# Another fixed order for the first fourteen steps of an attention and rational-MLP kernel

## The chip, the core and the metric

The kernel runs on one core of one Trainium2 chip. A core has five engines that work side by side, each through its own instructions in their order: TensorE (PE, matmuls; its weight loads are shown as PEld), VectorE (DVE), ScalarE (ACT), GpSimd (POOL) and SyncE (SP), which here issues nearly all of the DMAs. Engines wait for each other through semaphores. The metric is the device time of one execution in microseconds (us).

## What is computed

```python
# q, k, v: (4, 8, 768, 64)
k_sum = k.reshape(B, H, nb, 32, D).max(axis=3)
v_sum = v.reshape(B, H, nb, 32, D).mean(axis=3)
scores_l = where(|i - j| < 16, scale * q @ k.T, -1e9)
scores_s = scale * q @ k_sum.T + log(32)
a = softmax(concatenate([scores_l, scores_s]))
x = (a @ concatenate([v, v_sum])).transpose(0, 2, 1, 3).reshape(3072, 512)
h = x @ w_in                     # 512 -> 2048
P = a0 + a1*h + a2*h**2 + a3*h**3
Q = 1 + |b0|*|h| + |b1|*h**2
out = (P / (Q + 1e-6)) @ w_out   # 2048 -> 512
```

Each query sees its neighbours within 16 places and 24 block summaries of 32 keys. The result of the attention goes through a two-layer network with a rational function between the layers. The weights arrive as 64-bit numbers.

## The kernel before

**Tiling.** The 3072 rows are cut into six groups of 512 (`NG`), the hidden width of 2048 into sixteen chunks of 128 (`NFC`). One step is one chunk of one group, so there are 96 steps. In a step `moe1` (L390) multiplies the group's x by a chunk of `w_in` into a PSUM tile `h` (12 matmuls: high x high, high x low, low x high part), `gelu` (L402) evaluates the rational function and leaves a high and a low part, `gh` and `gl`, and three steps later (`LAG`) `moe2` (L432) multiplies these by the chunk of `w_out` into `po` (12 matmuls).

**Attention.** It is cut into 48 halves of 64 queries (`jj`). `whole(jj)` (L502) is a generator. Its pieces, one per call, are: score matmuls on PE (`sc`); masked maxima on DVE (`ss`, `sm`); four exponentials on ACT; a reciprocal on DVE (`sm`); the scaling of the probabilities on POOL (`ss`, four instructions); then, once PE has turned them (`turned`, L259, tile `pt`), a copy to SBUF on ACT (`pts`); value products on PE (`av`); a copy of the result on ACT (`x`). Halves 0 to 7, which make group 0, come before step 0; halves 8 to 15, which make group 1, start at steps 0, 1, 3, 4, 6, 7, 9 and 10 (`EARLY_HALF`); the rest follow in pairs after step 14.

**Weights.** `w_split(fc)` (L353) turns a 64-bit chunk into two FP32R parts, high and low. It is a generator of five pieces: a rescaling on ACT (`wr`), the low bits on POOL (`wr`), a merge on DVE (`wr`), the high part by a cast on ACT (`wearly` or `w`), the low part by a subtraction on DVE (`wearly` or `w`). The fifth piece also issues the load of the chunk four further on, into the buffer that it has just read (L386 to L388).

**The function between the layers.** `gelu` has five pieces: square, absolute value and a linear term on ACT (`sq` or `tq`, `ta`, `tu`); the denominator on DVE (`tq`, from `sq` in PSUM or from `tq` in SBUF); logarithm and exponential on ACT (`ta`); three fused operations on DVE (`gh`, `tq`, `tu`); a product on POOL (`gl`). Two further DVE operations on `tu`, which read `h` from PSUM, are called on their own (`products`, L406). The square goes to PSUM in steps 2, 5, 8, 11, 12 and 13 and to SBUF in the others (L414).

**What sets the order.** Three strings. `FIRST` (L48) is the order of the first loads: K keys with their block maxima, Q queries, S constants, F and G value tiles for the block means, W weight chunks, V values, A queries and keys of one half. `EARLY` (L49) orders the halves 0 to 7 and the first weight chunks: s scores and maxima, e the exponentials to the scaling, v block means, p or P the turning with the copy on ACT or DVE, c or C the value products, m the means, k a copy of the block maxima, w a piece of `w_split`. `STEP` (L56) is walked once per step after that step's `moe1`: a letter and a distance back (for w: ahead) name what makes its next piece. g is `gelu`, q the two products, h a half, w a chunk, k the copy of block maxima into `kw`, l and a loads of values and of queries with keys, u reductions of the next batch's keys and their loads, P the second layer with the turning (`moe2`), v block means of the second batch. In steps 0 to 13 (`NSTRICT`) each of PE, DVE, ACT and POOL keeps exactly the order in which the text issues its instructions (`Kept`, L78). SP isn't held by this. From step 14 on, a planner orders the work.

Of the kernel before, what the change touches and what calls it, by code (L numbers as in the profile page):

```python
# [18 lines left out]
B, H, S, D = 4, 8, 768, 64  # L19
# [25 lines left out]
LAG = 3  # L45
SOFF = 12
NWARM = 6
FIRST = "K0 Q0 K1 K2 K3 S F Q1 W0 V0 V1 V2 V3 V4 V5 V6 V7 W1 A8 A9 W2 W3 G"  # L48
EARLY = ("s0 s1 e0 s2 e1 s3 v0 v1 s4 e2 e3 P0 e4 v2 v3 s5 P1 s6 v4 v5 w0 w0 e5 w0 s7 P2 m0 w0 w0 C0 e6 P4 P3 e7 c2 c1 p5 P6 C3 P7 k8 w1 w1 c5 c4 w1 c7 k9 c6 w1 w1 w2 w2")  # L49
AVGW = NK + NB - 4  # L50
NLATE = 4
NSTG = 8
EARLY_HALF = (0, 1, 3, 4, 6, 7, 9, 10)
NSTRICT = NFC - 2
CROSS = 1
STEP = "h3 k0 h0 l0 h1 a0 w2 h1 g1 h3 h0 u w3 g0 w2 g0 q0 h0 w2 g1 w3 q0 P2 v h2 g0"  # L56
NHALF = NT // HQ


# [1 line left out]
def tile_kernel(ctx, tc, qw_in, kraw, kwin, vpad, vred, wio, a, b, cmask, cident, cavg, out):  # L61
# [407 lines left out]
    for i in range(NWARM):  # L469
        pe.matmul(warm, zero[:, 0:P], zero, start=True, stop=True)  # L470
    for what in FIRST.split():
        n = int(what[1:] or 0)
# [34 lines left out]
    chains, by_dve = {}, set()  # L507
    for what in EARLY.split():
        kind, n = what[0], int(what[1:])
# [41 lines left out]
    for step in range(NG * NFC + LAG):  # L551
# [6 lines left out]
        if g < NG:  # L558
# [4 lines left out]
            queue.append((g, fc, (gh, gl)))  # L563
        for what in STEP.split() if strictly else ():
            kind, n = what[0], int(what[1:] or 0)
# [120 lines left out]
```

## Time and profile before

| | us |
|---|---|
| median of three runs | 651.43 (650.79 to 651.48) |
| span of the profiled execution | 647.9 |
| median above the span | 3.5 |
| start of the first h matmul, step 0 | 37.25 |
| start of the h matmuls of step 14 | 144.21 |

The page of the profile gives the span of its execution from the first to the last instruction; what lies around the span is not shown there, so the 3.5 us are simply the difference between the two rows. Over the whole span PE is busy for 624.7 us, DVE for 576.9, ACT for 459.0 and POOL for 257.4. These are averages over stages with different limits: the loads and halves 0 to 7 up to 37 us, the fourteen ordered steps up to about 148 us, and the planned steps after that. All instructions that go through `Kept` carry line L88, so they are told apart by the names of their tiles (output<-inputs). In a timeline a row gives the start, the time taken, the engine, the operation, the tiles and shapes, how many were merged, and in brackets the idle time before it with what ended it.

### The profile page before, as it was taken

How to read it: one execution, taken by the hardware profiler on the slowest of the kernel's cores; microseconds unless marked ns; L12 is line 12 of the kernel's file. 1: busy time of each engine (PE TensorE's matmuls, PEld its weight loads, DVE VectorE, ACT ScalarE, POOL GpSimd, SP SyncE). 2: the span in 40 equal slices, each digit the busy share in tenths (PEclk: the TensorE clock that was granted, in tenths of full speed). 3: DMA queues.
4: the chain of work that ended last, by engine and by line, in shares of the span. 5: the costliest groups of instructions: out<-in, count | busy, mean ns of one | idle time of the engine just before them, and what ended most of it. 6: DMA issues, size and time to landing. Idle time of an engine off the chain costs nothing.

```text
span 647.9 us, 11828 instructions
## 1 busy us (share of the span) xinstructions
PE 624.7 (96%) x4068; PEld 499.4 (77%) x4068; DVE 576.9 (89%) x1152; ACT 459.0 (71%) x1032; POOL 257.4 (40%) x350
## 2 busy tenths in 40 slices
PE   8998879988999999999999999999999999999997
PEld 5666657866788887788888778888788888888886
DVE  4699999999998989988999999988988888988885
ACT  3889869977677577767758677758767756765652
POOL 1855666754243235244233244333334232222221
PEclk9999979989999999999999999999999999999999
DMA  9997644403354435234424332314233110010001
GB/s 322 340 356 263 205 148 157 139 26 107 113 176 116 125 122 160 83 128 150 119 88 141 103 129 93 108 63 130 66 129 114 40 64 1 21 45 1 0 2 65
DMA packets 51559, 77.00 MB, mean 119 GB/s; under 512 B 6068, under 2 KB 33076, under 8 KB 49580
## 3 DMA queue, kind: packets, MB, share of 16 engines
q1 hardware_dynamic: 50796, 75.80, 36.1%
q8 instruction: 32, 0.52, 0.3%
q10 hardware_dynamic: 576, 0.25, 0.1%
q0 software_dynamic: 128, 0.20, 0.1%
q14 instruction: 27, 0.22, 0.1%
HBM read 61.31 MB, written 14.73 MB: 117 GB/s over the span
## 4 chain that ended last, share of the span: by engine, by line
PE 51%; DVE 29%; ACT 7%; issue 6%; POOL 6%; DMA 1%; SPq 0%; DVEq 0%; POOLq 0%
PE po L88 24%; PE h L88 22%; DVE tu L88 10%; DVE tq L88 7%; DVE gh L88 4%; POOL ss L88 4%; ACT ss L88 3%; PE av L88 2%; DVE xl L88 2%; PE sc L88 2%; ACT ta L88 2%; DVE ss L88 2%; DVE ks L88 1%; DMA kres<-in_kraw_dram 1%; PE pt L88 1%
## 5 line engine op out<-in xcount | busy, mean ns | idle before, releaser
L88 POOL TENSOR_TENSOR gl<-tu,ta 128x512 fp32r<-128x512 f32 x96 | 129.1, 1345 | 298.9 <-DVE tu L88 159.6
L88 POOL TENSOR_SCALAR ss<-ss,sm 128x120 f32<-128x120 f32 x192 | 95.2, 513 | 81.6 <-DVE sm L88 79.5
L88 ACT ACTIVATE ta<-tq,cs 128x512 f32<-128x512 f32 x96 | 69.7, 726 | 76.3 <-DVE tq L88 74.7
L88 PE MATMUL po<-wearly,gh 128*128 128x512 f32 x384 | 122.8, 401 | 0.0
L88 PE MATMUL po<-w,gh 128*128 128x512 f32 x384 | 121.7, 398 | 0.0
L88 PE MATMUL h<-xh,wearly 128*128 128x512 f32 x384 | 96.1, 392 | 1.6 <-DVE sm L88 1.1
L88 PE MATMUL h<-xh,w 128*128 128x512 f32 x384 | 95.0, 389 | 0.0
L88 PEld LDWEIGHTS h<-xh,wearly 128*128 128x128 f32 x384 | 71.9, 188 | 18.7 <-ACT wr L88 1.3
L88 ACT ACTIVATE ss<-ss,sm 128x120 f32<-128x120 f32 x192 | 73.2, 384 | 15.4 <-DVE sm L88 15.2
L88 PEld LDWEIGHTS h<-xh,w 128*128 128x128 f32 x384 | 72.0, 188 | 15.2 <-ACT x L88 0.2
L88 PEld LDWEIGHTS po<-w,gh 128*128 128x128 f32 x384 | 71.3, 190 | 16.0 <-issue 1.7
L88 PEld LDWEIGHTS po<-wearly,gh 128*128 128x128 f32 x384 | 70.6, 191 | 16.2 <-issue 2.2
L88 DVE SCALAR_TENSOR_TENSOR gh<-tu,cs,ta 128x512 fp32r<-128x512 f32 x96 | 73.2, 762 | 9.2 <-ACT ta L88 1.2
L88 PE MATMUL po<-w,gl 128*128 128x512 f32 x192 | 75.4, 393 | 0.0
L88 PE MATMUL po<-wearly,gl 128*128 128x512 f32 x192 | 75.4, 393 | 0.0
L88 DVE SCALAR_TENSOR_TENSOR tu<-tu,cs,tq 128x512 f32<-128x512 f32 x96 | 72.9, 760 | 2.5
L88 ACT ACTIVATE tu<-h,cs 128x512 f32<-128x512 f32 x96 | 74.7, 778 | 0.0
L88 DVE SCALAR_TENSOR_TENSOR tu<-tu,cs,h 128x512 f32<-128x512 f32 x96 | 71.3, 743 | 2.3
L88 DVE SCALAR_TENSOR_TENSOR tq<-tq,gh 128x512 f32<-128x512 f32 x96 | 66.3, 691 | 3.0
L88 ACT ACTIVATE ta<-h,cs 128x512 f32<-128x512 f32 x96 | 65.2, 679 | 3.0 <-POOL gl L88 2.9
L88 DVE TENSOR_TENSOR tu<-tu,h 128x512 f32<-128x512 f32 x96 | 64.9, 676 | 0.0
L88 ACT ACTIVATE ta<-ta 128x512 f32<-128x512 f32 x96 | 60.9, 634 | 2.8
(73 smaller groups left out, 925.3 us busy)
## 6 DMA issues: line engine op xcount, KB each, us to landing
wr<-in_wio_dram SPq DMA_DIRECT2D x15, 1024.0 KB
cross<-tb SPq DMA_DIRECT2D x32, 256.0 KB
vw<-in_vpad_dram SPq DMA_DIRECT2D x42, 192.0 KB
kw<-in_kwin_dram SPq DMA_DIRECT2D x40, 192.0 KB
pts<-cross SPq DMA_DIRECT2D x96, 64.0 KB
out_dram<-o SPq DMA_DIRECT2D x24, 256.0 KB
qw<-in_qw_dram SPq DMA_DIRECT2D x40, 128.0 KB
kr<-in_kraw_dram SPq DMA_DIRECT2D x12, 384.0 KB
```

Source lines behind the costliest of these rows:

```text
L88: out = getattr(self.engine, name)(*args, **kw)
```

## The change

Only the three strings change.

```diff
-FIRST = "K0 Q0 K1 K2 K3 S F Q1 W0 V0 V1 V2 V3 V4 V5 V6 V7 W1 A8 A9 W2 W3 G"
-EARLY = ("s0 s1 e0 s2 e1 s3 v0 v1 s4 e2 e3 P0 e4 v2 v3 s5 P1 s6 v4 v5 w0 w0 e5 w0 s7 P2 m0 w0 w0 C0 e6 P4 P3 e7 c2 c1 p5 P6 C3 P7 k8 w1 w1 c5 c4 w1 c7 k9 c6 w1 w1 w2 w2")
+FIRST = "K0 Q0 K1 K2 K3 Q1 S F W0 V0 V1 V6 V2 V4 V5 A9 W1 V7 V3 A8 W2 W3 G"
+EARLY = "s0 s1 e0 s2 s6 e1 s3 s4 P0 v0 v1 e2 e3 e4 v2 v3 s5 P1 v4 v5 w0 w0 e5 w0 s7 P2 m0 w0 w0 C0 e6 P4 P3 e7 c2 c1 k8 p5 P6 C3 w1 P7 w1 c5 c4 w1 c6 c7 k9 w1 w1 w2 w2"
-STEP = "h3 k0 h0 l0 h1 a0 w2 h1 g1 h3 h0 u w3 g0 w2 g0 q0 h0 w2 g1 w3 q0 P2 v h2 g0"
+STEP = "k0 h3 w1 h2 h0 w2 P2 w1 w3 h3 g1 h0 g0 l0 q0 g1 g0 q0 h1 w2 u h0 a0 w3 v g0 h2"
```

Read by engine, a step s changes as follows (a chunk or half is named by its number; s-1 is the step before).

| engine | order before | order after |
|---|---|---|
| PE | h(s), av(s-3), sc(s), pt(s-2) with po(s-3), block means | the same |
| DVE | reciprocal(s-1), merge(s+2), gh tq tu (s-1), maxima(s), reduction, denominator(s), product(s), subtraction(s+2), product(s) | subtraction(s+1), merge(s+2), gh tq tu (s-1), maxima(s), product(s), denominator(s), product(s), reciprocal(s-1), reduction |
| ACT | x(s-3), rescaling(s+3), square to linear (s), cast(s+2), exponentials(s), pts(s-2), logarithm and exponential (s) | rescaling(s+3), x(s-3), square to linear (s), cast(s+2), exponentials(s), logarithm and exponential (s), pts(s-2) |
| POOL | scaling(s-1), gl(s-1), low bits(s+3) | scaling(s-2), gl(s-1), low bits(s+3) |

A chunk's subtraction, and with it the load of a later chunk, moves from step fc-2 to step fc-1, and the scaling of a half from the step after its scores to the second step after, in which PE also turns it.

## The prediction

> **What bounds the kernel now.** First the stretches of time, by busy time of each engine (start and end, length, then busy us of each engine with its instructions, granted clock, DMA share, GB/s):
>
> ```profile
> 60.00:80.00 20.00, 17.46 (x103) 13.41 (x104) 19.86 (x39) 17.13 (x40) 9.51 (x10) 1.00 0.67 222
> ...
> 175.00:644.00 469.00, 465.94 (x2855) 381.42 (x2844) 419.47 (x808) 322.27 (x712) 159.04 (x231) 1.00 0.28 89
> ```
>
> The third figure after the length is DVE. In this sample of the ordered steps it works for 19.86 of 20 us, PE for 17.46 and ACT for 17.13. After 175 us PE works for 465.94 of 469 us. So the ordered steps are bound by DVE, with PE and ACT not far behind, and what comes later by PE. A microsecond gained in the ordered steps therefore brings every later PE instruction forward by a microsecond; nothing in the tail waits for anything else long enough to swallow it.
>
> If DVE is already busy, can an order alone gain anything? Only if its instructions take longer than they need. The groups by line and shape for 37 to 165 us give the mean in ns after the busy time:
>
> ```profile
> L88 DVE TENSOR_TENSOR w<-wr,w 128x1024 fp32r<-128x1024 f32 x7 | 10.6, 1510 | 0.3 <-ACT w L88 0.2
> L88 DVE TENSOR_TENSOR wearly<-wr,wearly 128x1024 fp32r<-128x1024 f32 x7 | 10.5, 1501 | 0.0
> L88 DVE SCALAR_TENSOR_TENSOR tq<-tq,cs,ta 128x512 f32<-128x512 f32 x9 | 9.9, 1101 | 0.6 <-ACT ta L88 0.6
> L88 DVE COPY kw<-ks 128x96 f32<-128x96 f32 x3 | 1.5, 486 | 0.0
> ```
>
> Now DVE's timeline. The first rows run with POOL idle, the rows at 59.16, 66.79 and 122.83 do not:
>
> ```profile
> 42.12 0.75 DVE L88 SCALAR_TENSOR_TENSOR tq<-tq,cs,ta 128x512 f32<-128x512 f32 x1
> 42.78 0.68 DVE L88 TENSOR_TENSOR tu<-tu,h 128x512 f32<-128x512 f32 x1
> ...
> 59.16 2.07 DVE L88 TENSOR_TENSOR wearly<-wr,wearly 128x1024 fp32r<-128x1024 f32 x1
> ...
> 64.44 0.75 DVE L88 SCALAR_TENSOR_TENSOR tu<-tu,cs,tq 128x512 f32<-128x512 f32 x1
> ...
> 66.79 1.60 DVE L88 SCALAR_TENSOR_TENSOR tq<-tq,cs,ta 128x512 f32<-128x512 f32 x1
> 68.31 0.67 DVE L88 TENSOR_TENSOR tu<-tu,h 128x512 f32<-128x512 f32 x1
> 68.91 1.21 DVE L88 TENSOR_TENSOR wearly<-wr,wearly 128x1024 fp32r<-128x1024 f32 x1
> 70.05 0.73 DVE L88 SCALAR_TENSOR_TENSOR tu<-tu,cs,h 128x512 f32<-128x512 f32 x1
> ...
> 70.79 1.19 DVE L88 SCALAR_TENSOR_TENSOR wr<-wr 128x1024 int32<-128x1024 int32 x1
> 71.90 0.74 DVE L88 SCALAR_TENSOR_TENSOR gh<-tu,cs,ta 128x512 fp32r<-128x512 f32 x1
> ...
> 74.08 0.27 DVE L88 CUSTOM_DVE_ANT_0 ss<-sc,mask 128x120 f32<-128x120 f32 x1
> ...
> 74.89 0.95 DVE L88 TENSOR_REDUCE ks<-kr 128x24 f32<-128x768 f32 x1
> 75.75 0.79 DVE L88 SCALAR_TENSOR_TENSOR tq<-tq,cs,ta 128x512 f32<-128x512 f32 x1
> ...
> 86.53 1.23 DVE L88 SCALAR_TENSOR_TENSOR wr<-wr 128x1024 int32<-128x1024 int32 x1
> ...
> 110.60 1.23 DVE L88 SCALAR_TENSOR_TENSOR wr<-wr 128x1024 int32<-128x1024 int32 x1 [0.39 <-POOL wr L88]
> ...
> 122.83 1.65 DVE L88 SCALAR_TENSOR_TENSOR tq<-tq,cs,ta 128x512 f32<-128x512 f32 x1
> ```
>
> And POOL's own rows:
>
> ```profile
> 13.92 1.38 POOL L88 TENSOR_SCALAR ss<-ss,sm 128x120 f32<-128x120 f32 x4 [13.47 <-DVE sm L88]
> ...
> 59.02 1.12 POOL L88 TENSOR_SCALAR wr<-wr 128x1024 int32<-128x1024 uint8 x1
> 65.37 1.30 POOL L88 TENSOR_TENSOR gl<-tu,ta 128x512 fp32r<-128x512 f32 x1 [5.23 <-DVE tu L88]
> 66.76 1.09 POOL L88 TENSOR_SCALAR wr<-wr 128x1024 int32<-128x1024 uint8 x1
> 71.04 3.69 POOL L88 TENSOR_SCALAR ss<-ss,sm 128x120 f32<-128x120 f32 x4 [3.19 <-DVE sm L88]
> ...
> 76.07 1.47 POOL L88 TENSOR_SCALAR wr<-wr 128x1024 int32<-128x1024 uint8 x1
> ...
> 122.65 1.29 POOL L88 TENSOR_TENSOR gl<-tu,ta 128x512 fp32r<-128x512 f32 x1
> ```
>
> The reader is to see a pattern. POOL's `wr` began at 59.02 and DVE's subtraction, which reads two SBUF tiles, at 59.16: 2.07 us instead of 1.21, ending 1.09 after `wr` ended at 60.14. `tq` at 66.79 began just after a `wr` and took 1.60 instead of 0.75; at 122.83 it fell behind `gl` and took 1.65. At 75.75 `tq` was first: it took 0.79, and `wr` was stretched to 1.47. So of a long POOL instruction and a DVE instruction with two SBUF inputs, the later one waits. Operations on `h` in PSUM (0.67, 0.73) don't show it. [...]
>
> Last, two of the things that DVE waited for in 37 to 155 us (total, times, longest); the other two, 0.6 for `ta` and 0.2 for `w`, stand in the groups above:
>
> ```profile
> DVE wr L88 <- POOL wr L88: 1.3, 3, 0.5
> ...
> DVE ss L88 <- PE sc L88: 0.4, 1, 0.4
> ```
>
> The whole pot is: `tq` 9 x (1.10 - 0.75) = 3.2; subtractions 7 x (1.501 - 1.21) + 7 x (1.510 - 1.21) = 4.1; waits 1.3 + 0.6 + 0.4 + 0.2 = 2.5; the three `kw` copies at most 3 x 0.49 = 1.5. Sum 11.3 us.
>
> **The change, part by part.** No instruction is added or removed. The prices of DVE, from start to start in the rows above with POOL out of the way: subtraction 1.14 (68.91 to 70.05), merge 1.11, `gh`, `tq`, `tu` together 2.18 (71.90 to 74.08), maxima 0.81, reduction 0.86, `tq` denominator 0.66 (42.12 to 42.78), product 0.60 (68.31 to 68.91), the second product with a reciprocal 0.74 (70.05 to 70.79), of which I give the reciprocal 0.08.
>
> *Order of DVE and POOL in a step.* I lay the new order out from the start of the subtraction. With maxima: merge at 1.14, `gh` 2.25, end of `tu` 4.5, maxima 4.43, first product 5.24, denominator 5.84, second product 6.50, next step 7.24. POOL's `gl` follows `tu` by about 0.2 (`tu` of 64.44 ended at 65.19, `gl` began at 65.37), so 4.7 to 6.0. The denominator at 5.84 meets its last 0.15 us only, which costs nothing, since after a block it needs some 0.55 (122.83 + 1.65 less 122.65 + 1.29). That is what "maxima and product before the denominator" buys: 3.2 us to 0.1, if those 1.4 us stay in front of it. `wr` then waits for the denominator (6.6) and ends 1.0 later, 7.6, as at 76.07 to 77.54. The next subtraction, wanted at 7.24, ends 1.09 after that: 0.2 late. Without maxima: denominator at 5.03 from PSUM, next subtraction at 6.4, `wr` 6.1 to 7.2: 0.6 late. In steps 1 to 4 the reduction (0.86) now stands last and covers `wr`: nothing late. Steps 5, 8, 11, 12, 13 have no maxima, 6, 7, 9, 10 have: 5 x 0.6 + 4 x 0.2 = 3.8 us remain of the 4.1.
>
> *Waits.* The merge's wait for `wr` (1.3) goes, since the subtraction now stands ahead of it; that of the denominator for `ta` (0.6) is covered by the product before it (0.60); the subtraction's wait for the cast (0.2) by a whole step. The 0.4 in step 0 stays, its order is the same. Gain 2.1. The `kw` copies: no gain taken, 0 to 1.5 possible, since they now open a step beside the end of `wr`.
>
> *A chunk finished one step later.* One subtraction less in step 0, one more at step 14, where DVE has 419 of 469 us to do: nothing. Its load is issued later by up to a step, some 7 us, and must be there two steps on, some 14 us. Of SP's queue the waits for 30 to 150 us show
>
> ```profile
> SPq L251 <- PE av L88: 33.0, 6, 11.8
> ```
>
> A megabyte at the 222 GB/s of the table takes 4.7 us. I take nothing, but 11.8 + 4.7 would be 2.5 us late if a value load stood ahead of it.
>
> *PE and ACT.* From the chain that ended last (start, us, what):
>
> ```profile
> 96.33 0.62 PE av L88 x16
> 96.95 0.97 PE sc L88 x16
> 97.91 2.95 PE po L88 x12
> ...
> 103.59 0.11 PE pt L88
> ...
> 106.81 2.75 PE h L88 x12
> ...
> 110.23 0.37 ACT x L88
> ...
> 117.94 0.34 ACT x L88
> ```
>
> A PE step with everything: 0.62 + 0.97 + 3.22 (103.59 to 106.81, turning and `po`) + 2.75 = 7.6; without turning 7.3; without `av` and `sc` 6.0: 20.9 for three. ACT's full step is 7.7 (110.23 to 117.94), the others about 7.2 and 5.7: 20.6. DVE's three are 7.24 + 7.24 + 6.4 + 1.0 of remaining blocks = 21.9, where it now takes 24.1 (merges of 86.53 and 110.60, three steps apart). DVE stays the longest, with 1.0 us in front of PE. The copy `pts` now comes last on ACT and `av` waits for it; the square-to-linear run needs `x` copied first. By the rows that leaves the linear term ready some 0.6 us before its product asks for it. I take 0, bounded by 0 and 0.4 a full step, 1.6 in all.
>
> *Loads and halves 0 to 7.* The same work. Scores of half 6 come earlier on PE, its exponentials do not; the second queries pass ahead of 1.5 MB of value tiles that are used later. Taken as 0, bounds ±1 (the waits before PE in that stretch are each under 1 us).
>
> Sum: 3.1 + 0.3 + 2.1 = 5.5 us. Against the span: 647.9 - 5.5 = 642.4; the median shown lies 3.5 above the span, carried unchanged: **645.9 us**.
>
> **The rivals.**
>
> *More than that.* If `wr` starts before the subtraction is due in all steps, 3.8 more goes, and `kw` 1.5: 640.6. Against it: `wr` is held back by the denominator.
>
> *The blocks only move: no change.* POOL's `wr` can cost DVE at most one full block a step, 0.86 (row 59.16). Steps 1 to 13 in full: 11.2 us against 3.2 + 4.1 + 2.1 = 9.4 removed. Half a block more than I laid out per step gives 651.4 - 5.5 + 13 x 0.43 = 651.5. What speaks for it: the margin at the denominator is 0.2 us.
>
> *Slower: PE waits for the moved scaling.* Its queue is `wr`, then the scaling, with the turning of the same half in the same step on PE, and `po` and the next `h` behind it. PE has 24.1 - 20.9 = 3.2 us to spare in three steps, which hold two turnings; above 1.6 us of waiting for each the period is longer than before. At 2 us: 20.9 + 4 = 24.9, so 0.8 x 4.5 periods more than now, **655.0**. Against it: the scaling starts at about 0.1 to 0.4 of the step and, at 3.7 us, ends by 4.1, and only its first quarter must be there when the turning starts at about 3.
>
> Long waits of PE cost more:
>
> ```profile
> 86.61 1.86 PE L88 MATMUL sc<-kw,qw 64*64 64x120 f32 x16 [3.60 <-DVE kw L88]
> ```
>
> After 3.60 us of idleness these scores took 1.86 instead of the 0.97 above. [...]
>
> *Slower in another way: the scalings block DVE.* They now stand beside the subtraction and the merge. If each quarter (0.35, a fourth of the 1.38 at 13.92) started first and held DVE up, 8 halves x 1.38 = 11.0 us would come on top: 656.9. Against it: beside the scaling at 71.04 the `gh` at 71.90 and its followers kept their spacing. [...]
>
> *A late load.* It doesn't do what it says where the chunk's data arrive late: one or two waits of 2.5 us leave 648 to 651.
>
> **How the numbers follow.** A measurement of this kernel can tell about 0.2%, 1.3 us. My forecast, 645.9 with its own range of 643.5 to 648.5: 0.42. More (640 to 643.5): 0.16. A late load or part of the gain lost behind step 14 (648.5 to 650.1): 0.12. Blocks only move, 650.1 to 652.7: 0.12. Slower, 655 by PE's waits: 0.13; 657 by the scalings: 0.05. Faster 0.70, same 0.12, slower 0.18. The range: 640.6, the bottom of the pot, to 654; this leaves out about half the slower cases and a little below.
>
> **What would show it.** In the changed profile: `tq<-tq,cs,ta` near 0.75 to 0.85; subtractions still near 1.45 to 1.5; no wait of `wr` on DVE for POOL; three ordered steps about 22 us; `h` of step 14 some 5.5 us earlier than 144.21; the stretch after it as long as before. Wrong: waits of PE's `pt` for POOL `ss`, of ACT's `wr` for its load, `tq` still above 1.0, or a first `h` that moves by more than 1 us.

## The result, and the profile after

| | before | after |
|---|---|---|
| median (lowest to highest, runs) | 651.45 us (650.79 to 651.59, 4) | 646.92 us (645.66 to 648.14, 4) |
| ratio after / before, 95% interval | | 0.9937 [0.9912, 0.9961] |
| span of the profiled execution | 647.9 us | 643.6 us, its own time 645.66 |
| first `gh` to fourteenth `gh` on DVE | 102.22 us (46.37 to 148.59) | 97.50 us (46.69 to 144.19) |

The change saves 4.5 us in the median and 4.3 in the span. The last row is the measure used below: DVE makes `gh` once in each step, so from the first to the fourteenth lie thirteen ordered steps, without what the start of an execution adds before them.

The stretches of time show where the gain sits: start and end, length, then busy us of PE, its weight loads, DVE, ACT and POOL with their instructions, granted clock, DMA share, GB/s. Kernel before, four steps and then nine:

```profile
46.37:80.38 34.01, 29.80 (x182) 21.55 (x179) 33.73 (x64) 30.47 (x64) 21.43 (x21) 1.00 0.71 243
80.38:148.59 68.21, 62.70 (x416) 49.00 (x415) 65.26 (x113) 56.61 (x112) 43.91 (x40) 0.92 0.35 116
```

The changed kernel, the same steps, and the planned part behind them:

```profile
46.69:80.01 33.32, 29.73 (x170) 20.71 (x164) 31.94 (x65) 29.60 (x63) 22.11 (x19) 0.90 0.80 260
80.01:144.19 64.18, 60.12 (x394) 46.42 (x392) 63.55 (x113) 55.71 (x110) 47.26 (x42) 1.00 0.37 127
...
175.00:640.00 465.00, 461.61 (x2809) 377.80 (x2807) 414.81 (x790) 318.83 (x703) 157.74 (x230) 1.00 0.28 88
```

DVE's busy time falls by 1.79 us in the first four steps, but their length by only 0.69: idle time of DVE, which had been 0.28, is 1.38. In the nine steps behind, busy time falls by 1.71 and idle time from 2.95 to 0.63, and the length by 4.03. From 175 us on PE still works nearly all the time.

The groups of the changed kernel by shape, 37 to 158 us (busy us, mean ns of one, idle before), against 1510, 1501, 1101 and 486 before:

```profile
L88 DVE TENSOR_TENSOR w<-wr,w 128x1024 fp32r<-128x1024 f32 x7 | 10.7, 1527 | 0.0
L88 DVE TENSOR_TENSOR wearly<-wr,wearly 128x1024 fp32r<-128x1024 f32 x7 | 8.5, 1217 | 0.1
L88 DVE SCALAR_TENSOR_TENSOR tq<-tq,cs,ta 128x512 f32<-128x512 f32 x9 | 6.9, 769 | 0.0
...
L88 DVE COPY kw<-ks 128x96 f32<-128x96 f32 x3 | 1.8, 597 | 0.0
```

The denominator (`tq`) has lost its stretch. The seven early subtractions (`wearly`) have lost theirs, the seven later ones (`w`) have not, and the small copies `kw` became longer. The timeline says why. DVE's rows:

```profile
84.34 0.83 DVE L88 COPY kw<-ks 128x96 f32<-128x96 f32 x1
85.08 1.21 DVE L88 TENSOR_TENSOR wearly<-wr,wearly 128x1024 fp32r<-128x1024 f32 x1
...
98.55 0.75 DVE L88 SCALAR_TENSOR_TENSOR tq<-tq,cs,ta 128x512 f32<-128x512 f32 x1
...
99.96 1.40 DVE L88 TENSOR_TENSOR w<-wr,w 128x1024 fp32r<-128x1024 f32 x1
...
106.66 1.87 DVE L88 TENSOR_TENSOR w<-wr,w 128x1024 fp32r<-128x1024 f32 x1
```

and POOL's:

```profile
52.09 4.48 POOL L88 TENSOR_SCALAR ss<-ss,sm 128x120 f32<-128x120 f32 x4
...
83.98 1.12 POOL L88 TENSOR_SCALAR wr<-wr 128x1024 int32<-128x1024 uint8 x1
...
97.41 1.30 POOL L88 TENSOR_TENSOR gl<-tu,ta 128x512 fp32r<-128x512 f32 x1 [4.67 <-DVE tu L88]
98.79 1.50 POOL L88 TENSOR_SCALAR wr<-wr 128x1024 int32<-128x1024 uint8 x1
...
106.33 1.13 POOL L88 TENSOR_SCALAR wr<-wr 128x1024 int32<-128x1024 uint8 x1
```

In a step with maxima `gl` ends at 98.71 and `tq`, at 98.55, is clean; `wr` stretches behind `tq` to 100.29 and delays the subtraction of 99.96 by 0.2. In a step without maxima `wr` starts at 106.33, 0.3 before the subtraction, which then takes 1.87. Step 6 opens with the copy `kw`, which takes the blow, 0.83 where it takes 0.20 unhindered (row of 94.57 in the kernel before), and the subtraction at 85.08 is clean.

Last, what PE and DVE waited for from 37 to 152 us (total, times, longest). First DVE:

```profile
DVE ss L88 <- PE sc L88: 1.0, 2, 0.5
DVE gh L88 <- ACT ta L88: 0.3, 1, 0.3
DVE tu L88 <- ACT tu L88: 0.3, 1, 0.3
```

and PE, with a wait that was not there before:

```profile
PE pt L88 <- POOL ss L88: 6.8, 8, 2.2
```

Four of those eight waits, 3.6 of the 6.8 us, stand in one place, the turning in step 2. PE's timeline:

```profile
52.52 0.32 PE L88 MATMUL pt<-ident,ss 128*120 128x128 f32 x1 [0.74 <-POOL ss L88]
55.08 0.47 PE L88 MATMUL pt<-ident,ss 128*120 128x128 f32 x1 [2.24 <-POOL ss L88]
55.85 0.47 PE L88 MATMUL pt<-ident,ss 128*120 128x128 f32 x1 [0.30 <-POOL ss L88]
56.62 0.47 PE L88 MATMUL pt<-ident,ss 128*120 128x128 f32 x1 [0.30 <-POOL ss L88]
56.88 3.62 PE L88 MATMUL vf<-vf,kres 128*120 128x512 f32 x4
...
59.52 3.31 PE L88 MATMUL h<-xh,wearly 128*128 128x512 f32 x8
```

The four scalings, 4.48 us from 52.09 on, are awaited one by one. After that the block means (`vf`) take 3.62 us instead of 1.98 (row of 47.05 in the same timeline), and the next `h` 3.31 instead of 2.40 (48.46). The granted clock is 0.50 from 54.58 to 61.41 us, which makes the 0.90 of the first stretch, and this is the source of DVE's new waits in step 3.

### The profile page after: what moved, and what is told of

The parts are those of the page before. It is cut to its first block, busy times and chain, and to the rows that moved or that the text cites. A ratio compares the mean times of both kernels' runs of the same rounds, so it can differ in the third digit from the quotient of the medians.

```text
span 643.6 us, 11833 instructions
## 1 busy us (share of the span) xinstructions
PE 623.1 (97%) x4068; PEld 497.2 (77%) x4068; DVE 573.3 (89%) x1152; ACT 459.1 (71%) x1032; POOL 259.7 (40%) x350
## 4 chain that ended last, share of the span: by engine, by line
PE 62%; DVE 19%; POOL 7%; ACT 5%; issue 4%; DMA 2%; SPq 0%; DVEq 0%; POOLq 0%
PE po L88 28%; PE h L88 27%; DVE tu L88 7%; POOL ss L88 5%; DVE tq L88 4%; PE sc L88 3%; PE av L88 3%; DVE gh L88 2%; DVE xl L88 2%; ACT ta L88 1%; PE vf L88 1%; DVE ss L88 1%; DMA kres<-in_kraw_dram 1%; POOL gl L88 1%; ACT ss L88 1%
## 5 line engine op out<-in xcount | busy, mean ns | idle before, releaser
L88 POOL TENSOR_SCALAR ss<-ss,sm 128x120 f32<-128x120 f32 x192 | 100.8, 544 | 61.8 <-DVE sm L88 59.1
```

Source lines behind the costliest of these rows:

```text
L88: out = getattr(self.engine, name)(*args, **kw)
```

## The experiments

Theory: a DVE instruction with two SBUF inputs waits for a POOL instruction that reads SBUF, whole instruction for whole instruction, and the order within a step decides which pairs meet. Rivals: the gain comes from the start (loads and halves 0 to 7), or from finishing chunks a step later; or what costs is not the reading but a dependence on POOL's result, or POOL being busy at all. All lengths below are from the first `gh` to the fourteenth in the one profiled execution of each kernel. A ratio is taken against the runs of the kernel before that were made beside that kernel; their medians were 651.45 us for the first result, 651.40 for the four runs from the new start to the denominator first, 651.18 for the repeat and the three from the chunk in its step to the eight matmuls, and 650.06 for the last four.

| run | length us | time us (lowest to highest, runs) | ratio to before, 95% interval |
|---|---|---|---|
| before | 102.22 | 651.45 | |
| changed | 97.50 | 646.92 | 0.9937 [0.9912, 0.9961] |
| changed, again | 97.22 | 646.93 (645.21 to 654.09, 12) | 0.9939 [0.9909, 0.9970] |
| new start alone | 102.91 | 652.18 (650.34 to 657.29, 12) | 1.0014 [0.9985, 1.0043] |
| new step order alone | 97.33 | 645.54 (645.27 to 645.60, 6) | 0.9907 [0.9870, 0.9944] |
| before, product ahead of denominator | 102.25 | 651.57 (649.31 to 654.54, 12) | 1.0003 [0.9978, 1.0028] |
| changed, denominator first | 99.94 | 652.91 (651.12 to 656.77, 12) | 1.0021 [0.9993, 1.0050] |
| changed, chunk finished in its step | 96.33 | 647.67 (644.03 to 653.98, 12) | 0.9928 [0.9901, 0.9955] |
| changed, means before turning | 96.08 | 645.29 (644.00 to 650.20, 12) | 0.9915 [0.9893, 0.9937] |
| changed, eight warming matmuls | 97.27 | 646.13 (645.73 to 647.85, 6) | 0.9925 [0.9898, 0.9953] |
| before, POOL writes zeros | 96.58 | 645.60 (1) | |
| changed, POOL writes zeros | 94.47 | 642.97 (1) | |
| means before turning, eight warming | 96.34 | 645.77 (645.10 to 646.98, 6) | 0.9928 [0.9914, 0.9942] |
| the same, chunk finished in its step | 96.26 | 646.83 (645.34 to 647.20, 6) | 0.9939 [0.9924, 0.9954] |

**The two halves of the change.** The kernel before with the new strings `FIRST` and `EARLY` and the old `STEP`:

```diff
-FIRST = "K0 Q0 K1 K2 K3 S F Q1 W0 V0 V1 V2 V3 V4 V5 V6 V7 W1 A8 A9 W2 W3 G"
+FIRST = "K0 Q0 K1 K2 K3 Q1 S F W0 V0 V1 V6 V2 V4 V5 A9 W1 V7 V3 A8 W2 W3 G"
...
```

> FIRST and EARLY of the changed kernel, STEP of the one before. Theory (the gain comes from the order inside the ordered steps, where a DVE instruction with two SBUF inputs no longer starts behind a long POOL instruction): 651.4 within 1.5, tq<-tq,cs,ta again near 1.1 us. Rival (the loads and halves 0 to 7 bring the gain): about 647, first h matmul earlier than 37.25.

and, the other way round, the old start with the new `STEP`:

```diff
-STEP = "h3 k0 h0 l0 h1 a0 w2 h1 g1 h3 h0 u w3 g0 w2 g0 q0 h0 w2 g1 w3 q0 P2 v h2 g0"
+STEP = "k0 h3 w1 h2 h0 w2 P2 w1 w3 h3 g1 h0 g0 l0 q0 g1 g0 q0 h1 w2 u h0 a0 w3 v g0 h2"
```

> FIRST and EARLY of the kernel before, STEP of the changed one. Theory: all of the gain, 646.9 within 1.5, tq<-tq,cs,ta near 0.77 us. Rival (loads and halves 0 to 7): about 651.

The denominator's group in the first of them, and then in the second:

```profile
L88 DVE SCALAR_TENSOR_TENSOR tq<-tq,cs,ta 128x512 f32<-128x512 f32 x9 | 11.4, 1269 | 0.0
```

```profile
L88 DVE SCALAR_TENSOR_TENSOR tq<-tq,cs,ta 128x512 f32<-128x512 f32 x9 | 7.0, 774 | 0.0
```

The new start alone has the old length and no gain in time, with a `tq` that is even longer than the 1.1 us expected; the new step order alone has the whole gain. The start is worth nothing that these runs can tell.

**One pair exchanged.** In the kernel before the product is put ahead of the denominator and nothing else:

```diff
-STEP = "h3 k0 h0 l0 h1 a0 w2 h1 g1 h3 h0 u w3 g0 w2 g0 q0 h0 w2 g1 w3 q0 P2 v h2 g0"
+STEP = "h3 k0 h0 l0 h1 a0 w2 h1 g1 h3 h0 u w3 g0 w2 q0 g0 h0 w2 g1 w3 q0 P2 v h2 g0"
```

> The kernel before with one swap in STEP: the first product ahead of the denominator (q0 before the second g0). Theory: tq<-tq,cs,ta falls to 0.75 to 0.9 in the steps with maxima, but POOL's low bits then run into the subtraction, which follows at once and grows; net gain 0 to 1.5 us, 650 to 651.5. Rival (the swap alone is the gain, blocks are simply gone): about 648.

The two groups:

```profile
L88 DVE TENSOR_TENSOR w<-wr,w 128x1024 fp32r<-128x1024 f32 x7 | 13.4, 1908 | 0.0
...
L88 DVE SCALAR_TENSOR_TENSOR tq<-tq,cs,ta 128x512 f32<-128x512 f32 x9 | 8.7, 965 | 0.0
```

`tq` fell by 9 x 0.14 = 1.2 us and the `w` subtractions rose by 7 x 0.40 = 2.8 (`wearly` gave 0.7 back), DVE's waits became shorter, and the length is the same to 0.03 us. The block that was not let run out found the next instruction with two SBUF inputs, `w`, 1908 ns instead of 1510. In the changed kernel the opposite exchange, denominator ahead of product:

```diff
-STEP = "k0 h3 w1 h2 h0 w2 P2 w1 w3 h3 g1 h0 g0 l0 q0 g1 g0 q0 h1 w2 u h0 a0 w3 v g0 h2"
+STEP = "k0 h3 w1 h2 h0 w2 P2 w1 w3 h3 g1 h0 g0 l0 g0 q0 g1 q0 h1 w2 u h0 a0 w3 v g0 h2"
```

> The changed kernel with the swap undone: the denominator ahead of the first product (g0 before q0). Theory: in the eight steps with maxima tq<-tq,cs,ta ends about 0.55 later than it could, near 1.25 us, the subtraction behind it is no longer blocked in those steps; loss 1.5 to 3 us, 648.5 to 650. Rival (the earlier subtraction and the later scaling bring the gain, not the place of the denominator): 646.9 within 1.

```profile
L88 DVE SCALAR_TENSOR_TENSOR tq<-tq,cs,ta 128x512 f32<-128x512 f32 x9 | 10.2, 1137 | 0.6 <-ACT ta L88 0.6
L88 DVE TENSOR_TENSOR w<-wr,w 128x1024 fp32r<-128x1024 f32 x7 | 9.7, 1387 | 0.0
```

`tq` is back above 1.1 us and the ordered steps are 2.4 us longer. The median rose by more, 6.0 us, beyond the 1.5 to 3 expected. The profiled execution took 655.29 us, and its span is 9.9 us longer than the changed kernel's: 4.0 of that lie before the first `h` (41.53 us instead of 37.51, see the last section), 2.4 in the ordered steps and 3.5 behind them. Why the planned part became longer was not tested, so only the 2.4 are put down to the exchange.

**The deferral alone.** Every chunk is finished in its step again, the rest of the new order stays:

```diff
-STEP = "k0 h3 w1 h2 h0 w2 P2 w1 w3 h3 g1 h0 g0 l0 q0 g1 g0 q0 h1 w2 u h0 a0 w3 v g0 h2"
+STEP = "k0 h3 h2 h0 w2 P2 w3 h3 g1 h0 g0 l0 q0 g1 g0 q0 h1 w2 u w2 h0 a0 w3 v g0 h2"
```

> The changed kernel with a chunk finished one step earlier again: its subtraction is now the last of a step instead of the first of the next, so that DVE's order from step to step is the same but for the chunk number. Theory: the step's delay is worth nothing, only the subtraction's place is: first to fourteenth gh 97.5 within 0.7 (one subtraction more falls into it, 1.1 us, at its begin, before the first gh), whole time as in the repeat within 1.5. Rival (finishing later gives slack to cast and load and is part of the gain): 1.5 us or more slower than the repeat, with waits of DVE for ACT's cast.

The time did not move beyond its scatter (647.67 against 646.93 in the repeat of the changed kernel beside it). The ordered steps became 0.9 us shorter than in that repeat, and their 96.33 us lie outside the 97.5 within 0.7 that was expected. The repeat, for the scatter of starts and times:

> The changed kernel once more, beside the next three on one chip. From the first gh of DVE to the fourteenth it needs 97.5 us (102.2 before); that will repeat within 0.5. The whole time also depends on the start: in executions whose PE clock falls to half between 10 and 20 us, the first h matmul comes some 4 us later. 645.5 to 647 if the start keeps its clock, 649 to 651 if not.

The 0.9 us are not the deferral's. The second and third of the thirteen steps together, in the repeat and then with each chunk finished in its step:

```profile
59.70:76.40 16.70, 16.04 (x97) 10.98 (x98) 16.07 (x28) 13.55 (x28) 10.70 (x10) 0.82 0.69 227
```

```profile
60.19:75.72 15.53, 14.72 (x90) 10.37 (x92) 15.39 (x28) 13.16 (x27) 11.05 (x10) 0.89 0.77 245
```

They differ by 1.17 us; over the last nine steps the kernel without the deferral is 0.3 us longer (64.42 against 64.13). PE's waits at the turning of step 2 are alike in both: the four turnings start 5.82, 7.26, 8.56 and 9.33 us after the first `gh` in the repeat, and 5.82, 7.25, 8.55 and 9.33 in the other. What differs is the granted clock behind them. It is 0.50 for 6.83 us in the repeat (58.92 to 65.75) and for 3.42 us without the deferral (62.39 to 65.81).

**Step 2.** If the awaited scaling eats what the first steps gain, work for PE ahead of the turning should give some back. The block means (`v`) are such work; they are put ahead of the second layer with its turning:

```diff
-STEP = "k0 h3 w1 h2 h0 w2 P2 w1 w3 h3 g1 h0 g0 l0 q0 g1 g0 q0 h1 w2 u h0 a0 w3 v g0 h2"
+STEP = "k0 h3 w1 h2 h0 w2 v P2 w1 w3 h3 g1 h0 g0 l0 q0 g1 g0 q0 h1 w2 u h0 a0 w3 g0 h2"
```

> The changed kernel with the block means (v) ahead of the turning (P2) in a step. In step 2 PE waits 3.3 us for the moved scaling, then runs at half clock, and DVE waits 0.3 to 0.5 us three times in step 3. Theory: the means fill that wait; first to fourteenth gh falls by 0.5 to 1.2 us from 97.5. Rival (DVE's queue hides this wait as well): 97.5 within 0.2.

PE's timeline in that kernel, the same place:

```profile
52.59 1.88 PE L88 MATMUL vf<-vf,kres 128*120 128x512 f32 x4
...
54.91 0.33 PE L88 MATMUL pt<-ident,ss 128*120 128x128 f32 x1 [0.34 <-POOL ss L88]
56.21 0.32 PE L88 MATMUL pt<-ident,ss 128*120 128x128 f32 x1 [0.98 <-POOL ss L88]
56.98 0.32 PE L88 MATMUL pt<-ident,ss 128*120 128x128 f32 x1 [0.45 <-POOL ss L88]
57.09 2.08 PE L88 MATMUL h<-xh,wearly 128*128 128x512 f32 x8
```

The means run while the first scalings are done; three waits of 1.77 us together are left of the four of 3.6, the granted clock stays at 1.00, and the next `h` takes 2.08 us instead of 3.31. First to fifth `gh` is 31.91 us (47.66 to 79.57), 1.41 less than in the changed kernel, and that is the whole difference of the two lengths; the waits of DVE in step 3 are gone from its list. So the four steps did lose 1.4 us at this one place. But they take 31.91 us also in the kernel that finishes each chunk in its step, where PE waits as long as in the repeat and only the stretch at half clock is shorter. The 1.4 us are thus the price of the long stretch at half clock, not of the waits alone. Five profiled executions with the means behind the turning have the long stretch of 6.8 us (the changed kernel, its repeat, the new step order alone, eight warming matmuls, zeros written) and one has the short one; with the means in front there is none here, and one of 3.4 us in each of the two kernels with eight warming matmuls. That the place of the means makes the difference is likely from this, but one profile of each kernel doesn't show it.

**What POOL does to DVE.** The direct test leaves POOL's instruction in its place and, nearly, its length, but lets it only write. It leaves out the low three bits of the weights' parts:

```diff
-            gps.tensor_scalar(l32, byte, 1.0 / 32, -15.5 / 32, op0=ALU.mult, op1=ALU.add)
+            gps.memset(l32, 0)
```

> The kernel before, with POOL's piece of a weight chunk (the low bits, `wr`, read from bytes) replaced by a POOL instruction of the same place that only writes zeros to the same tile and reads nothing; the low three bits of the weights' parts are left out by this. My theory (a DVE instruction with two SBUF inputs waits for a POOL instruction that reads SBUF, whole instruction for whole instruction): the subtractions fall from 1.50 to about 1.21 us, the merge no longer waits for POOL, `tq` keeps only what `gl` costs it, and from the first `gh` to the fourteenth on DVE it takes 96 to 99 us instead of 102.2. [...]

> The changed kernel with the same replacement (POOL's low bits of a chunk become a write of zeros; the low three bits of the weights' parts are left out). My theory: the subtractions of the steps without reduction fall from 1.40 to 1.87 us to 1.21, `tq` stays near 0.75, and the length from the first `gh` to the fourteenth falls from 97.5 to 93.5 to 95; beside the same replacement in the kernel before, 2 to 4 us remain, the part of `tq` that `gl` costs. [...]

In the kernel before with that edit, POOL's rows

```profile
58.54 1.07 POOL L88 MEMSET wr<- 128x1024 int32 x1
...
65.42 1.02 POOL L88 MEMSET wr<- 128x1024 int32 x1
...
126.64 1.27 POOL L88 TENSOR_TENSOR gl<-tu,ta 128x512 fp32r<-128x512 f32 x1
```

and DVE's beside them:

```profile
58.82 1.22 DVE L88 TENSOR_TENSOR wearly<-wr,wearly 128x1024 fp32r<-128x1024 f32 x1
...
65.60 0.74 DVE L88 SCALAR_TENSOR_TENSOR tq<-tq,cs,ta 128x512 f32<-128x512 f32 x1
...
127.27 1.73 DVE L88 TENSOR_TENSOR w<-wr,w 128x1024 fp32r<-128x1024 f32 x1
```

The subtraction of 58.82 begins inside a POOL instruction of 1.07 us that only writes, and takes its clean 1.22; the same subtraction took 2.07 us in the kernel before, inside a `wr` of 1.12 that reads. `tq` at 65.60 is clean as well. The subtraction of 127.27 falls into `gl`, which reads, and takes 1.73. For a DVE instruction with two SBUF inputs it is the reading instruction that costs, not POOL's work as such. Both rivals fall: POOL is still busy for 1.07 us there and the merge still takes its result, so either would have left the subtraction near 2.07; and the lengths of 96.58 and 94.47 us lie in the ranges of the theory. The copy `kw` doesn't fit this rule. It reads one SBUF tile only and was stretched by the reading `wr`, and in the changed kernel with the edit it still takes 0.59 us at 83.78, inside a writing instruction (83.27 to 84.31), though the subtraction behind it starts 0.10 us later and takes its clean 1.22. The reduction, also with one SBUF input, keeps its 0.92 when it begins inside a reading `wr` (59.04 in the changed kernel). Why the copy differs no run isolates. The groups of this kernel, then those of the changed kernel with the edit:

```profile
L88 DVE TENSOR_TENSOR w<-wr,w 128x1024 fp32r<-128x1024 f32 x7 | 9.7, 1384 | 0.0
L88 DVE SCALAR_TENSOR_TENSOR tq<-tq,cs,ta 128x512 f32<-128x512 f32 x9 | 9.7, 1076 | 0.0
```

```profile
L88 DVE TENSOR_TENSOR w<-wr,w 128x1024 fp32r<-128x1024 f32 x7 | 8.4, 1204 | 0.0
...
L88 DVE SCALAR_TENSOR_TENSOR tq<-tq,cs,ta 128x512 f32<-128x512 f32 x9 | 7.0, 782 | 0.1
```

Without a `wr` that reads, the old order loses 5.6 us of length and the new order 3.0. Of the 4.7 between the two orders 2.1 remain, 3.0 in the last nine steps (64.95 against 61.98) less 0.9 in the first four, where the new order still has its stretch at half clock. What remains is put down to `gl`, which hits `tq` and `w` in the old order (9.7 us each) and hardly in the new (7.0 and 8.4). The subtractions of the old order, too, fell only to 1.38 and 1.29 us, not to the 1.21 expected.

**More warming, and the edits together.** Eight warming matmuls in place of six, alone and with the means ahead of the turning, and the latter with the deferral undone:

```diff
-NWARM = 6
+NWARM = 8
```

> The changed kernel with eight instead of six warming matmuls (NWARM). Theory for the start: PE stays busy until the keys have landed, the clock no longer falls, first h matmul at 37.5 to 38.5 in every execution, 645.5 to 648 with a spread under 2 us. Rival (the late landing of the keys itself sets the start, the clock only follows): spread as before, first h as often at 41 to 42.

> The changed kernel with the block means ahead of the second layer in a step and with eight warming matmuls in place of six: the two edits that each came out a little faster alone. My theory (the means are DVE work that fills a gap, 1.4 us in the ordered steps; the longer warming keeps the start from falling to half clock in the executions in which it does): median 644 to 645.5, a narrower spread of the times than with six (under 3 us from lowest to highest), ratio to the kernel before 0.988 to 0.992. Rival (the spread of the start is not set by the warming): median 645 to 647 with a spread of 5 us or more.

> The one before with the weight chunks finished in the same step again, the deferral undone. My theory (the deferral is worth nothing, in either direction): ordered steps within 1 us of the run before this, time within 0.2% of it. Rival (the deferral covers the subtraction's wait for the cast or the late `wr`): 1 to 3 us longer, with waits of DVE for ACT's cast of 0.5 us or more in the ordered steps.

Warming changes no length. The times of the three kernels with eight scatter by 1.9 to 2.1 us, those with six that ran beside the first of these by 6 to 10 us (changed kernel again, chunk in its step, means first); but beside the other two the kernel before, with six, scattered by only 1.95 us (649.74 to 651.69), and the new step order alone, with six, by 0.33. So whether the warming narrows the times stays open. The two edits together came out at 645.77 us, above the 644 to 645.5 expected. The last two give the deferral no price in the ordered steps, 96.26 against 96.34 us; their times are 1.1 us apart in its favour, within their scatter. The lowest median of the study outside the zero-writing kernels is that of the means first, 645.29 us; its interval overlaps that of the changed kernel, so its times show no gain, and the 1.1 to 1.4 us of length are those of the stretch at half clock.

## Why the prediction was right, and where not

The forecast of 645.9 us lies 1.0 below the median measured, and by span 642.4 lies 1.2 below 643.6. The 3.5 us that were carried from span to median are 3.3 here. Only 2.06 of them lie between this execution's own time and its span; the rest is that the profile caught an execution faster than the median. It did so before, too (the other runs of the kernel before lie 1.8 us above their spans), and that this repeated is luck. Step by step:

**DVE bounds the ordered steps, and POOL's reading instructions stretch it.** Right, and shown by the zero-writing pair. Three ordered steps take 22.24 us (merges of 86.21 and 108.45), as forecast. Two readings behind it were loose. The rows given for operations on `h` in PSUM, 68.31 and 70.05, ran while POOL was idle; one that ran inside a `wr` (76.07 to 77.54) shows the same:

```profile
76.46 0.68 DVE L88 TENSOR_TENSOR tu<-tu,h 128x512 f32<-128x512 f32 x1
```

And the 1.38 us for the four scalings at 13.92, from which the 657 is worked out, don't belong to an idle DVE: until 14.6 it took maxima of scores in PSUM.

**`tq`, -3.1.** Measured 9.9 to 6.9 us, -3.0. Right. One of nine is still hit (0.96 at 67.15).

**Subtractions, -0.3.** Measured 21.1 to 19.2 us for the fourteen, -1.9, but the prediction's 3.8 us of remaining blocks were well sized: 7 x (1.527 - 1.21) = 2.2 remain on `w`, 0.6 + 0.3 fell on the `kw` copies that open steps 6 and 7, in front of the subtraction, and 0.35 on the merge of two half chunks in step 13 (1.72 us where 1.37 is clean in the kernel before). That is 3.5. The gain came out larger than 0.3 because a part of it fell outside the subtractions, and there it was paid: `kw`, taken as 0 with a possible gain, cost 0.6 us more than before over the thirteen steps, and the half chunks' merge 0.35. Together -0.95 in place of -0.3.

**Waits, -2.1.** The merge's wait for POOL (1.3) and the denominator's for `ta` (0.6) went as said. Idle time of DVE over the thirteen steps fell only from 3.23 to 2.01, -1.2, since step 3 got new ones: 0.5 for scores, 0.3 for `ta`, 0.3 for the linear term. They come from PE, the next point.

**PE, taken as 0.** This is the step that failed. The rival in which PE waits for the moved scaling was half there, with 6.8 us in eight waits. It gave 655 with 2 us at every turning; measured were 3.6 us at the turning of step 2 and 3.2 at the other four together, and only the first reached DVE. The prediction let a turning start at about 3 us of the step, amid the second layer's matmuls. In step 2 the second layer, which comes three steps behind, hasn't begun, so the four turnings stand alone and PE waits for each scaling. In the kernel before the granted clock was 0.50 from 85.4 us, still inside the wait of 3.60 us that the prediction shows, to 92.1. Here no wait was longer than 2.24 us, with short matmuls between them, and the clock fell to 0.50 for 6.8 us all the same. The price is 1.4 us, and it hangs on this stretch at half clock: the same waits with half the stretch cost the first four steps nothing. With 1.4 taken off, the length would be 96.1 us, 6.1 gained; with it 4.7 were, instead of 5.5.

**Scalings block DVE, the 657.** Hardly. The scalings are stretched (4.59 us for four at 100.39, 1.38 at 13.92), and the DVE instructions beside them are longer by little: from the first `gh` to the fourteenth the mean of the merge went from 1202 to 1223 ns, that of `gh` from 744 to 761, that of `tq<-tq,gh` from 693 to 720; 12, 13 and 13 of them make 0.8 us against the 11.0 of that rival. Why POOL gives way here and not with `wr` no run isolates. The terms as measured, 3.0 + 0.95 + 1.2 less these 0.8, make 4.4 of the 4.7 us; that the subtractions brought more than forecast offset in part what the waits and the scalings cost, and for this too the forecast was lucky.

**Deferral, loads and halves 0 to 7, at nothing.** Right: the runs with the new start or the new step order alone show the old or the new length to within 0.7 us, the one without the deferral to within 1.2, which are those of the half clock, and none of the waits of 37 to 152 us in the changed kernel is for a late load but one of POOL, 0.9 us at the start of step 0, ahead of the first `gh` (which comes 0.3 us later than before).

**`h` of step 14, 5.5 us earlier.** Wrong: 144.21 to 141.56, 2.65 earlier. PE was further ahead of DVE there in the kernel before, and lost that lead by step 17, waiting for the low part of the second group's x, which DVE writes. PE's waits from 150 to 170 us, before:

```profile
PE h L88 <- DVE xl L88: 2.0, 2, 1.8
```

and changed:

```profile
PE h L88 <- DVE xl L88: 0.4, 1, 0.4
```

By step 17 `h` starts at 159.81 instead of 164.30, 4.5 us earlier, and from there to the end it is 483.8 us against 483.6. The DVE gain showed on PE where PE next waited for DVE (4.5 us), not at the next step's start (2.65).

## What to carry to other kernels

When DVE is the bound and its instructions have two lengths, look up what POOL does in the long ones. In this kernel a DVE instruction with two SBUF inputs that starts inside a long POOL instruction which reads SBUF ends late by about what is left of that one (at 59.16 in the kernel before 2.07 us instead of 1.21, 0.86 late with 0.98 left). To save the time, let the block meet DVE work that it doesn't hold up (here products on PSUM, 0.68 us inside a `wr`, a maximum, 0.28 inside `gl` at 65.52 in the kernel before, or the reduction, 0.92 inside a `wr`, but not the small copy, 0.83 instead of 0.20), or let POOL's instruction not read (1.22); exchanging two vulnerable instructions only moved it (0.03 us of length). A piece of work moved closer to its consumer needs other work ahead of the consumer: the price came from one place where it ran short, not from the mean wait, and by way of the clock that fell behind it (0.50 for 6.8 us). So look at the granted clock, too, before a difference of a microsecond is put down to an order.

## What the runs showed of the hardware that was not expected

Executions of the same kernel start differently. The changed kernel, first profile, the warming and the stretch of 12 to 14 us:

```profile
1.46 8.05 PE L88 MATMUL warm<-zero 128*128 128x512 f32 x12 [1.46 <-DVE cs L88]
...
12.00:14.00 2.00, 2.00 (x64) 2.00 (x61) 1.58 (x16) 1.97 (x12) 0.09 (x1) 1.00 1.04 383
```

and its repeat:

```profile
1.46 6.81 PE L88 MATMUL warm<-zero 128*128 128x512 f32 x12 [1.46 <-DVE cs L88]
...
12.00:14.00 2.00, 2.00 (x36) 2.00 (x33) 0.77 (x9) 1.69 (x10) 0.00 (x0) 0.50 1.06 390
```

The same six warming matmuls, which the profile shows as twelve instructions, took 8.05 us in one and 6.81 in the other. Where they ended early, PE was busy for only 1.41 and 1.37 us of the two stretches of 2 us from 8 on, the granted clock was 0.50 from 12 to 20 us, half as many matmuls ran, and the first `h` came at 42.32 us instead of 37.51. Of the first eight experiments above, up to the zero-writing ones, five show a first `h` at 41.07 to 42.83 and three at 37.44 to 38.45, with both starts under the old strings of the start as under the new; so a few microseconds of a single run's time say nothing of an edit in the ordered steps. An early end of the warming is not enough for it: with 7.08 us the clock stayed at 1.00 in the kernel with the means first (first `h` at 38.45). What makes the starts differ no run isolates; the 4.8 us between these two first `h` are 0.7% of the span of 643.6.
